# Local attention in half chunks: 64x64 score tiles over 128 keys, global keys apart

## The chip, the cores and the metric

The kernel runs on one core of a Trainium2 chip. The metric is the device time of one launch in microseconds, the median of several runs. TensorE (PE) does the matrix products, VectorE (DVE) and ScalarE (ACT) the elementwise work, and all transfers are issued from the SP queue onto the core's 16 DMA engines.

## What is computed

The reference is one sparse attention followed by two feed-forward layers. The attention has 4 batches, 8 heads, 512 local and 32 global tokens of 64 elements; a local query sees the 32 global keys and the local keys at most 32 positions away, and a global query sees everything:

```python
s_g = scale * q_g @ concat(k_g, k_l).T          # 32 x 544 per head
out_g = softmax(s_g) @ concat(v_g, v_l)
s_ll = where(|i - j| <= 32, scale * q_l @ k_l.T, -1e9)
s_l = concat(scale * q_l @ k_g.T, s_ll)         # 512 x 544, at most 97 of them alive
out_l = softmax(s_l) @ concat(v_g, v_l)
x = concat(out_g, out_l)                        # 2176 tokens x 512
xn = x / rms(x) * rms_g
x = (silu(xn @ w_gate) * (xn @ w_val)) @ w_out  # 512 -> 1536 -> 512
out = (s * relu(x @ w_in)**2 + b) @ w_out2      # 512 -> 2048 -> 512
```

The weights come as float64 and are split into a high and a low float32r part; each feed-forward product is three matmuls (high by high, high by low, low by high).

## The kernel before, in words

The 2176 tokens go through both layers in five groups: three of 512 (the local tokens of batches 0, 1, 2) and two of 320. For each group the main loop goes over 12 slots of the first layer and 16 of the second. `mm3` issues the three matmuls (lines 606 to 608) and is called from `emit_first` (tile m, or m from y) and `emit_second` (tile acc). In the first group's slots the weights are converted beside the products: `conv` takes raw blocks (tile wr), one or two at a time, through ACT and DVE, and the result goes to DRAM (wsc), from where later groups load it.

The attention of batch 0 is done in `start`, before the first products: eight pieces of two chunks (a chunk is 128 queries of two heads), each with `S_` (scores, mask, exponential), `N_` (division by the sum), `T_` (transposes of the probabilities) and `V_` (product with the values). Each piece's queries, keys and values come in one tile s_w. Score and transpose results alternate between the PSUM tiles acc0 and at (two banks each, through `nb`); `V_` takes the one-bank tiles m, of which there are two.

The attention of batches 1 to 3 is cut into 12 units (a batch and two heads), in `unit_steps`. Their steps are queued, and `tick`, called after every group of three matmuls, sends the next one when its time has come. So TensorE's order has short attention groups between long rows of feed-forward matmuls. A unit has two score steps (`sc(0)`, `sc(2)`, line 262), two transpose steps (`st_t`, lines 340 and 341), and one value step (`st_v`, line 354). Every second unit also does the global queries of two units (`st_g` lines 272 and 273, `st_tg` lines 309 and 311, `st_gv` line 329). All of these use one PSUM tile, at, of two banks.

In the score step a chunk's keys are 224 columns: 32 before the chunk, 32 behind it, the 32 global ones, 128 of its own. The two heads lie on partitions 0 to 63 and 64 to 127, so one matmul has 64 rows and 128 output columns, and the heads' results go to different banks. The probabilities, 224 columns a chunk and head, are transposed in two overlapping pieces of 128, and the value step has two matmuls a chunk and head, of 128 rows and 64 output columns each, the two heads side by side. Every float32 matmul of the attention is two instructions on the chip (lines 262, 354, 329, 272, 273); a transpose is one.

The order on each engine is made at build time by a list scheduler with a timing model; `in_turn` keeps a step's matmuls in the order in which they are written.

Of the kernel before, what the change touches and what calls it, by code (L numbers as in the profile page):

```python
# [20 lines left out]
ST = SG + SL  # L21
# [3 lines left out]
KW = 224  # L25
# [30 lines left out]
NMAX = max(GN)  # L56
W_BUFS = 5
# [4 lines left out]
def attn_moe_kernel(ctx: ExitStack, tc: tile.TileContext, s0, q, k, v, w1, w2, cst, out):  # L62
# [47 lines left out]
    pg = cp.tile([128, 64 + ST], F32, name="pg")  # L110
# [104 lines left out]
    def load_u(i):  # L215
        if i >= len(UNITS) or i in raw_u:
            return
        b, p, loc = UNITS[i]
        vr = at_p.tile([128, 4, 2, 2, D], F32, tag="vr", name="vr", bufs=2)
        e = ST if loc else SG  # L220
        qr = at_p.tile([128, ST], F32, tag="qr", name="fq")
        kr = kr_p.tile([128, 4, KW], F32, tag="kr", name="fk")
# [15 lines left out]
    def unit_steps(i):  # L238
# [15 lines left out]
        def sc(c0):  # L254
            qr, kr, vr = raw_u[i]
            bk = banks("at")
            mms = []
            for c in (c0, c0 + 1):
                o = SG + 128 * c
                for h in range(2):  # L260
                    x = slice(64 * h, 64 * h + 64)
                    mms.append(PE.matmul(bk[:, h, (c - c0) * KW:(c - c0 + 1) * KW], lhsT=qr[x, o:o + 128], rhs=kr[x, c]))  # L262
            in_turn(mms)
# [4 lines left out]
        def st_g():  # L268
# [3 lines left out]
            mms = [PE.matmul(bk[64 * e:64 * e + 64, 0], lhsT=qf[:, e], rhs=kr[e][:, :, 96:KW]) for e in range(2)]  # L272
            mms += [PE.matmul(bk[64 * e:64 * e + 64, 1, 0:SG], lhsT=qf[:, e], rhs=kr[e][:, 0, 64:96]) for e in range(2)]
            in_turn(mms)
            neg_scaled(pg[:, 96:96 + SL], bk[:, 0], zw, gm[:, 1:2])
            neg_scaled(pg[:, 64:96], bk[:, 1, 0:SG], zeros[:, 0:SG], gm[:, 0:1])
            V.tensor_tensor(out=gm[:, 2:3], in0=gm[:, 0:1], in1=gm[:, 1:2], op=ALU.min)

        def st_e(cs, g):
# [7 lines left out]
            if g:  # L287
                gm = S["gm"]
                A.activation(out=pg[:, 64:64 + ST], in_=pg[:, 64:64 + ST], func=AF.Exp, scale=-1.0,
                             bias=gm[:, 2:3], accum_out=gm[:, 3:4])  # L290

        def st_r():
# [8 lines left out]
            V.tensor_scalar(out=pg[:, 64:64 + ST], in0=pg[:, 64:64 + ST], scalar1=gm[:, 4:5], scalar2=None, op0=ALU.mult)  # L301

        def st_n(c):
            for h in range(2):
                norm_eng(pm[:, c, h], pm[:, c, h], S["rs"][:, c, h:h + 1], "A" if h else "V")

        def st_tg():
            bk = banks("at")
            mms = [PE.transpose(bk[:, 0, 0:128], pg[:, 0:128], ident)]
            for c in range(4):  # L310
                mms.append(PE.transpose(bk[:, 1, 128 * c:128 * c + 128], pg[:, 96 + 128 * c:224 + 128 * c], ident))
# [7 lines left out]
        def st_gv():  # L319
# [3 lines left out]
            for e in range(2):  # L323
                vr = raw_u[i - 1 + e][2]
                for c in range(5):
                    for h in range(2):
                        o = bk[64 * h:64 * h + 64, SG * e:SG * e + SG]
                        lhs = vr[:, c, 1, h] if c < 4 else vr[:, 0, 0, h]
                        mms.append(PE.matmul(o, lhsT=lhs, rhs=t[:, (c + 1) % 5, e, h], start=(c == 0), stop=(c == 4)))  # L329
# [5 lines left out]
        def st_t(c0):  # L335
            bk = banks("at")
            mms = []
            for c in range(2):
                for h in range(2):
                    mms.append(PE.transpose(bk[:, c, 256 * h:256 * h + 128], pm[:, c0 + c, h, 0:128], ident))  # L340
                    mms.append(PE.transpose(bk[:, c, 256 * h + 128:256 * h + 256], pm[:, c0 + c, h, 96:KW], ident))  # L341
            in_turn(mms)
            t = pt_p.tile([128, 2, 2, 2, 128], F32, tag="pt", name="ptf")
            A.copy(out=t.rearrange("p c h t n -> p c (h t n)"), in_=bk)
            S["pt", c0] = t

        def st_v():
            bk = banks("at")[:, 0]
            vr = raw_u[i][2]
            mms = []  # L350
            for c in range(4):
                for ty in (1, 0):
                    for h in range(2):
                        mms.append(PE.matmul(bk[64 * h:64 * h + 64, 128 * c:128 * c + 128], lhsT=vr[:, c, ty, h],  # L354
                                             rhs=S["pt", c // 2 * 2][:, c % 2, h, ty], start=(ty == 1), stop=(ty == 0)))
            in_turn(mms)
            cpy("V", u_tile(b)[:, p], bk.rearrange("p (c n) -> p c n", c=4))
# [106 lines left out]
    def start():  # L464
# [3 lines left out]
        def ld(i):  # L468
            if not spare:
                t = w_p.tile([128, 2, 1216], F32, tag="w", name="s_w")  # L470
# [3 lines left out]
            rw.append((t[:, 0:256], t[:, 256:704].rearrange("p (c n) -> p c n", c=2),  # L474
                       t[:, 704:1216].rearrange("p (c t h d) -> p c t h d", c=2, t=2, h=2)))
# [20 lines left out]
        G.memset(pg[:, 0:64], 0.0)  # L496
# [13 lines left out]
        def S_(i):  # L510
# [3 lines left out]
            mms = []  # L514
            for c in range(2):
                for h in range(2):
                    x = slice(64 * h, 64 * h + 64)
                    mms.append(PE.matmul(bk[:, h, c * KW:(c + 1) * KW], lhsT=qr[x, 128 * c:128 * c + 128], rhs=kr[x, c]))
            in_turn(mms)
# [9 lines left out]
        def N_(i):  # L529
            V.tensor_scalar(out=st[i][:, 2], in0=st[i][:, 1], scalar1=1e-9, scalar2=None, op0=ALU.add)  # L530
            V.reciprocal(out=st[i][:, 2], in_=st[i][:, 2])
            for n in range(4):
                x = P[i % 4][:, n // 2, n % 2]
                norm_eng(x, x, st[i][:, 2, n:n + 1], "V")

        pts = {}

        def T_(i):
            bk = nb()
            mms = []  # L540
            for c in range(2):
                for h in range(2):
                    mms.append(PE.transpose(bk[:, c, 256 * h:256 * h + 128], P[i % 4][:, c, h, 0:128], ident))
                    mms.append(PE.transpose(bk[:, c, 256 * h + 128:256 * h + 256], P[i % 4][:, c, h, 96:KW], ident))
            in_turn(mms)
            t = pt_p.tile([128, 2, 2, 2, 128], F32, tag="pt", name="s_pt")
            A.copy(out=t.rearrange("p c h t n -> p c (h t n)"), in_=bk)
            pts[i] = t

        def V_(i):  # L550
            bk = one_bank()
            vr = rw[i][2]
            mms = []
            for c in range(2):
                for ty in (1, 0):
                    for h in range(2):
                        mms.append(PE.matmul(bk[64 * h:64 * h + 64, 128 * c:128 * c + 128], lhsT=vr[:, c, ty, h],
                                             rhs=pts[i][:, c, h, ty], start=(ty == 1), stop=(ty == 0)))
            in_turn(mms)
            o = 2 * (i // 4)  # L560
            cpy("A", u_tile(0)[:, i % 4, o:o + 2], bk[:, 0:256].rearrange("p (c n) -> p c n", c=2))
# [145 lines left out]
def _masks():  # L707
    qi = np.arange(128)[:, None]
    m = np.zeros((128, 3, KW), np.float32)
    for t in range(3):  # L710
        pv = np.arange(32)[None] - 32
        nx = np.arange(32)[None] + 128
        ow = np.arange(128)[None]
        m[:, t, 0:32] = np.where((np.abs(qi - pv) <= 32) & (t != 0), 0.0, NEG)
        m[:, t, 32:64] = np.where((np.abs(qi - nx) <= 32) & (t != 2), 0.0, NEG)
        m[:, t, 96:224] = np.where(np.abs(qi - ow) <= 32, 0.0, NEG)
# [3 lines left out]
def _layout(inp):  # L720
# [6 lines left out]
    z = np.zeros((B, HP, 2, 32, D), f)  # L727
    ka = np.zeros((B, HP, 2, 4, KW, D), f)
# [55 lines left out]
```

## Time and profile before

| | us |
|---|---|
| median of 3 runs (lowest, highest) | 1008.27 (1006.88, 1008.33) |
| the profiled execution | 1005.52 |
| its span, first to last instruction | 1003.7 |
| PE busy / DVE busy / ACT busy in the span | 959.5 / 477.5 / 484.2 |

The profile names an instruction by line, engine, operation and tiles (out<-in). Matmuls are pipelined and the record of one reaches past the start of the next, so what a group of matmuls costs is read here from starts: from the start of the last foreign matmul before it to the start of the first one behind it.

### The profile page before, as it was taken

The page shows a single profiled execution, that of the slowest core. Times are in us where ns is not written, and L with a number is a line of the kernel's source. Part 1 is how long each engine was busy: PE and PEld are TensorE (multiplying, and loading weights), DVE is VectorE, ACT ScalarE, POOL GpSimd, SP SyncE. Part 2 cuts the span into 40 slices and gives each one's busy share as a digit, 9 for nine tenths or more (in the row PEclk, how much of TensorE's full clock was granted, in tenths as well). Part 3 has the DMA queues.
Part 4 walks back from the last instruction along what each step waited for, and adds up shares of the span by engine and source line. Part 5 has one row for each costly group of instructions (what it writes and reads, how often), then busy time and mean ns, then how long its engine had stood idle before and what let it go on. Part 6 is the DMA issues. An engine that isn't in the chain of part 4 may idle for free.

```text
span 1003.7 us, 14288 instructions
## 1 busy us (share of the span) xinstructions
PE 959.5 (96%) x5608; PEld 810.5 (81%) x5608; DVE 477.5 (48%) x1117; ACT 484.2 (48%) x906; POOL 0.8 (0%) x9
## 2 busy tenths in 40 slices
PE   6669999899989999999999999999999999999998
PEld 5447878677868878787877878777889999999998
DVE  6995887879854131334254141443252233421323
ACT  6996687768645152544346262643442342321222
POOL 0000000000000000000000000000000000000000
PEclk9888999899999999999999999999999999999999
DMA  9984789768864654436565554436578847898584
GB/s 372 372 299 170 295 336 348 255 222 300 305 222 163 256 191 174 157 132 214 206 222 193 228 192 168 155 130 227 189 263 324 328 170 288 320 371 303 178 328 153
DMA packets 41107, 243.82 MB, mean 243 GB/s; under 512 B 5072, under 2 KB 6096, under 8 KB 23120
## 3 DMA queue, kind: packets, MB, share of 16 engines
q1 hardware_dynamic: 41040, 242.91, 65.4%
q8 instruction: 44, 0.72, 0.3%
q14 instruction: 23, 0.19, 0.1%
HBM read 202.79 MB, written 40.11 MB: 242 GB/s over the span
## 4 chain that ended last, share of the span: by engine, by line
PE 81%; ACT 8%; DMA 5%; DVE 4%; issue 1%; SPq 0%; ACTq 0%; DVEq 0%
PE m L606 14%; PE m L607 14%; PE m L608 14%; PE acc L606 10%; PE acc L607 10%; PE acc L608 10%; DMA wr<-in_w_dram 4%; PE at L354 2%; PE at L262 2%; ACT ce L175 2%; ACT pm L285 2%; ACT cv L174 1%; PE at L340 1%; PE at L329 1%; PE at L341 1%
## 5 line engine op out<-in xcount | busy, mean ns | idle before, releaser
L607 PE MATMUL acc<-h,wt 128*128 128x512 f32 (+1 forms) x560 | 201.5, 361 | 0.0
L608 PE MATMUL acc<-h,wt 128*128 128x512 f32 (+1 forms) x560 | 200.4, 359 | 0.0
L606 PE MATMUL acc<-h,wt 128*128 128x512 f32 (+1 forms) x560 | 191.4, 362 | 0.9 <-DVE y L140 0.6
L606 PE MATMUL m<-x,wt 128*128 128x512 f32 (+2 forms) x496 | 177.7, 359 | 2.6 <-ACT x L134 2.6
L607 PE MATMUL m<-x,wt 128*128 128x512 f32 (+2 forms) x496 | 176.6, 356 | 0.2 <-DVE x L140 0.2
L608 PE MATMUL m<-x,wt 128*128 128x512 f32 (+2 forms) x496 | 176.0, 355 | 0.0
L606 PE MATMUL m<-y,wt 128*128 128x512 f32 (+1 forms) x320 | 116.5, 372 | 7.5 <-ACT y L134 5.1
L606 PEld LDWEIGHTS acc<-h,wt 128*128 128x128 f32 x560 | 103.8, 188 | 16.0 <-issue 1.5
L607 PEld LDWEIGHTS acc<-h,wt 128*128 128x128 f32 x560 | 105.4, 188 | 13.8 <-issue 0.8
L607 PE MATMUL m<-y,wt 128*128 128x512 f32 (+1 forms) x320 | 116.3, 364 | 0.0
L608 PEld LDWEIGHTS acc<-h,wt 128*128 128x128 f32 x560 | 105.4, 188 | 13.2 <-issue 0.2
L608 PE MATMUL m<-y,wt 128*128 128x512 f32 (+1 forms) x320 | 115.7, 362 | 0.0
L676 DVE TENSOR_TENSOR a<-sg,m 128x512 f32<-128x512 f32 (+1 forms) x60 | 36.4, 607 | 150.3 <-PE m L608 132.0
L606 PEld LDWEIGHTS m<-x,wt 128*128 128x128 f32 x496 | 93.9, 190 | 15.7 <-ACT x L134 3.0
L607 PEld LDWEIGHTS m<-x,wt 128*128 128x128 f32 x496 | 94.3, 190 | 12.5 <-issue 1.5
L608 PEld LDWEIGHTS m<-x,wt 128*128 128x128 f32 x496 | 94.3, 190 | 11.4 <-issue 0.8
L695 DVE SCALAR_TENSOR_TENSOR t<-m,ct,r 128x512 f32<-128x512 f32 (+1 forms) x80 | 53.1, 668 | 98.3 <-ACT r L694 97.9
L694 ACT ACTIVATE r<-m 128x512 f32<-128x512 f32 (+1 forms) x80 | 42.0, 532 | 99.6 <-PE m L608 99.3
L697 ACT ACTIVATE h<-t,ct 128x512 fp32r<-128x512 f32 (+1 forms) x80 | 52.4, 659 | 63.2 <-DVE t L695 42.4
L134 ACT CAST h<-a 128x512 fp32r<-128x512 f32 (+1 forms) x60 | 33.3, 555 | 96.6 <-DVE a L676 80.3
L698 DVE SCALAR_TENSOR_TENSOR h<-t,ct,h 128x512 fp32r<-128x512 f32 (+1 forms) x80 | 53.5, 669 | 48.7 <-ACT h L697 48.3
L606 PEld LDWEIGHTS m<-y,wt 128*128 128x128 f32 x320 | 59.9, 190 | 19.9 <-ACT y L134 6.6
(133 smaller groups left out, 1196.2 us busy)
## 6 DMA issues: line engine op xcount, KB each, us to landing
wt<-wsc SPq DMA_DIRECT2D x48, 1536.0 KB, 7.1
wt<-wsc SPq DMA_DIRECT2D x64, 1024.0 KB, 4.8
wr<-in_w_dram SPq DMA_DIRECT2D x68, 512.0 KB, 5.5
wsc<-wt SPq DMA_DIRECT2D x12, 1536.0 KB, 6.1
wsc<-wt SPq DMA_DIRECT2D x16, 1024.0 KB, 5.6
vr<-in_v_dram SPq DMA_DIRECT2D x16, 512.0 KB, 5.6
fk<-in_k_dram SPq DMA_DIRECT2D x16, 448.0 KB, 6.8
s_w<-in_s_dram SPq DMA_DIRECT2D x8, 608.0 KB, 9.9
```

Of the source, the lines that this page charges most:

```text
L134: A.copy(out=out_, in_=in_)
L175: A.copy(out=e.bitcast(I16), in_=odd)
L262: mms.append(PE.matmul(bk[:, h, (c - c0) * KW:(c - c0 + 1) * KW], lhsT=qr[x, o:o + 128], rhs=kr[x, c]))
L285: A.activation(out=pm[:, c, h], in_=pm[:, c, h], func=AF.Exp, scale=-1.0, bias=n2[:, c, h:h + 1], accum_out=S["sum"][:, c, h:h + 1])
L606: PE.matmul(out_, lhsT=wh, rhs=xh, start=first, stop=False)
L607: PE.matmul(out_, lhsT=wh, rhs=xl, start=False, stop=False)
L608: PE.matmul(out_, lhsT=wl, rhs=xh, start=False, stop=last)
L676: V.tensor_tensor(out=a[:, :N], in0=sg[:, :N], in1=vb[:, :N], op=ALU.mult)
L694: A.activation(out=r[:, :N], in_=hb[:, :N], func=AF.Relu)
L695: V.scalar_tensor_tensor(out=t[:, :N], in0=hb[:, :N], scalar=ct[:, C_S:C_S + 1], in1=r[:, :N], op0=ALU.mult, op1=ALU.mult)
L697: A.activation(out=h[:, 0, :N], in_=t[:, :N], func=AF.Identity, bias=ct[:, C_B:C_B + 1])
L698: V.scalar_tensor_tensor(out=h[:, 1, :N], in0=t[:, :N], scalar=ct[:, C_B:C_B + 1], in1=h[:, 0, :N].bitcast(F32), op0=ALU.add, op1=ALU.subt ...
```

## The change

A score tile becomes 64 queries by 160 keys: 128 local keys (32 before the half chunk, its own 64, 32 behind) and the 32 global ones. A chunk of two heads has four such tiles, by half `e` and head `h`; the halves go to different output partitions. The keys are laid out on the host for every half chunk (8 x 160 columns instead of 4 x 224), the values likewise (9 x 128 columns and 64 of the global values instead of 1024), and the local window is one transpose of 128 columns a chunk and head. The global probabilities of two chunks and two heads, 4 x 32 columns, are scaled by the new `glob` and transposed together as a fifth piece. In the value step the local products have 64 moving columns, one a half chunk and head, and the global ones have 32 rows, at four row positions. The value step's result lies in two banks instead of one; in `start` it takes its banks from `nb` instead of m. The piece loaded in `start` grows from 1216 to 1472 columns. The layout of pg (global queries) moves by 64 columns.

```diff
-KW = 224
+KW = 160
+VW = 9 * 128 + 64
+SW = 256 + 4 * KW + 4 * 128 + 64
...
+    def scores(bk, qr, kr, q0, cs):
+        mms = []
+        for n, c in enumerate(cs):
+            for e in range(2):
+                for h in range(2):
+                    x = slice(64 * h, 64 * h + 64)
+                    i = 2 * c + e
+                    mms.append(PE.matmul(bk[64 * e:64 * e + 64, h, n * KW:(n + 1) * KW],
+                                         lhsT=qr[x, q0 + 64 * i:q0 + 64 * i + 64], rhs=kr[x, i]))
+        in_turn(mms)
+
+    def glob(p, rs):
+        gl = pt_p.tile([128, 4, 32], F32, tag="gl", name="gl")
+        V.tensor_tensor(out=gl, in0=p.rearrange("p c h n -> p (c h) n")[:, :, 128:KW],
+                        in1=rs.rearrange("p (n o) -> p n o", o=1).broadcast_to((128, 4, 32)), op=ALU.mult)
+        return gl.rearrange("p n k -> p (n k)")
+
+    def transposes(bk, p, gl):
+        flat = bk.rearrange("p b n -> p (b n)")
+        mms = []
+        for c in range(2):
+            for h in range(2):
+                o = 128 * (2 * c + h)
+                mms.append(PE.transpose(flat[:, o:o + 128], p[:, c, h, 0:128], ident))
+        mms.append(PE.transpose(flat[:, 512:640], gl, ident))
+        in_turn(mms)
+        t = pt_p.tile([128, 5, 128], F32, tag="pt", name="ptf")
+        A.copy(out=t.rearrange("p a n -> p (a n)"), in_=flat[:, 0:640])
+        return t
+
+    def values(bk, vr, vg, pts):
+        mms = []
+        for c in range(2 * len(pts)):
+            t = pts[c // 2]
+            for e in range(2):
+                for h in range(2):
+                    i = 2 * c + e
+                    o = 128 * (c // 2) + 64 * e
+                    mms.append(PE.matmul(bk[64 * h:64 * h + 64, c % 2, o:o + 64],
+                                         lhsT=vr[:, 128 * i + 64 * h:128 * i + 64 * h + 64],
+                                         rhs=t[:, 2 * (c % 2) + h, 64 * e:64 * e + 64], start=(c < 2 and e == 0), stop=False))
+        for c in range(2 * len(pts)):
+            t = pts[c // 2]
+            for h in range(2):
+                x = slice(32 * (2 * (c % 2) + h), 32 * (2 * (c % 2) + h) + 32)
+                o = 128 * (c // 2)
+                mms.append(PE.matmul(bk[64 * h:64 * h + 64, c % 2, o:o + 128], lhsT=vg[x], rhs=t[x, 4],
+                                     start=False, stop=(c // 2 == len(pts) - 1), tile_position=(x.start, 64 * h)))
+        in_turn(mms)
...
         def st_n(c):
+            if not c % 2:
+                S["gl", c] = glob(pm[:, c:c + 2], S["rs"][:, c:c + 2].rearrange("p c h -> p (c h)"))
             for h in range(2):
-                norm_eng(pm[:, c, h], pm[:, c, h], S["rs"][:, c, h:h + 1], "A" if h else "V")
+                norm_eng(pm[:, c, h, 0:128], pm[:, c, h, 0:128], S["rs"][:, c, h:h + 1], "A" if h else "V")
...
         def st_v():
             bk = banks("at")
             vr = raw_u[i][2]
+            values(bk, vr, vr[:, VW - 64:VW], [S["pt", 0], S["pt", 2]])
+            cpy("V", u_tile(b)[:, p].rearrange("p (c b) n -> p c b n", b=2),
+                bk[:, :, 0:256].rearrange("p b (c n) -> p c b n", c=2))
...
         def V_(i):
-            bk = one_bank()
+            bk = nb()
             vr = rw[i][2]
+            values(bk, vr, vr[:, 512:576], [pts[i]])
             o = 2 * (i // 4)
-            cpy("A", u_tile(0)[:, i % 4, o:o + 2], bk[:, 0:256].rearrange("p (c n) -> p c n", c=2))
+            cpy("A", u_tile(0)[:, i % 4, o:o + 2], bk[:, :, 0:128])
```

## Rows read from the trace of the kernel before

**Rows 1.** The page: PE's busy share, and PE's granted clock in 40 slices.

```profile
PE 959.5 (96%) x5608; PEld 810.5 (81%) x5608; DVE 477.5 (48%) x1117; ACT 484.2 (48%) x906; POOL 0.8 (0%) x9
PEclk9888999899999999999999999999999999999999
```

**Rows 2.** Windows: stretch, length, busy PE, PEld, DVE, ACT, POOL, clock, DMA, GB/s.

```profile
20.00:40.00 20.00, 13.87 (x126) 10.02 (x124) 19.95 (x78) 17.97 (x45) 0.00 (x0) 1.00 1.03 413
...
60.00:80.00 20.00, 12.16 (x61) 9.56 (x60) 19.65 (x54) 18.22 (x40) 0.00 (x0) 0.76 0.84 312
...
460.00:560.00 100.00, 100.00 (x515) 80.68 (x512) 38.67 (x82) 43.48 (x77) 0.00 (x0) 1.00 0.60 219
```

**Rows 3.** Timeline of PE, a value step between products: start, length, instruction, count.

```profile
403.49 0.39 PE L608 MATMUL m<-x,wt 128*128 128x512 f32 x1
403.72 0.39 PE L606 MATMUL m<-x,wt 128*128 128x512 f32 x1
404.04 1.97 PE L354 MATMUL at<-ptf,vr 128*64 128x128 f32 x32
405.93 0.50 PE L607 MATMUL m<-x,wt 128*128 128x512 f32 x1
```

**Rows 4.** Timeline of PE, a transpose step, the first and the last of eight.

```profile
397.60 0.27 PE L340 MATMUL at<-ct,pm 128*128 128x128 f32 x1
...
398.36 0.27 PE L341 MATMUL at<-ct,pm 128*128 128x128 f32 x1
```

**Rows 5.** Timeline of PE, a score step between products.

```profile
410.82 0.39 PE L607 MATMUL m<-x,wt 128*128 128x512 f32 x1
411.14 1.03 PE L262 MATMUL at<-fk,fq 64*128 64x224 f32 x8
412.10 0.50 PE L608 MATMUL m<-x,wt 128*128 128x512 f32 x1
```

**Rows 6.** Timeline of PE, a value step of the global queries between products.

```profile
475.97 0.39 PE L607 MATMUL m<-y,wt 128*128 128x512 f32 x1
476.29 1.36 PE L329 MATMUL at<-pgt,vr 128*64 128x32 f32 x40
477.58 0.50 PE L608 MATMUL m<-y,wt 128*128 128x512 f32 x1
```

**Rows 7.** Groups by form: line, engine, operation, shapes, count | busy us, mean ns | idle before.

```profile
L229 DVE CUSTOM_DVE_ANT_0 pm<-at,ct 128x224 f32<-128x224 f32 x108 | 35.7, 385 | 37.8 <-PE at L262 37.8
...
L236 DVE TENSOR_SCALAR pm<-pm,rs 128x224 f32<-128x224 f32 x48 | 13.1, 331 | 0.3
...
L547 ACT COPY s_pt<-acc 128x1024 f32<-128x1024 f32 x7 | 7.0, 995 | 1.3 <-PE acc L544 1.3
...
L229 DVE CUSTOM_DVE_ANT_0 pg<-at,zeros 128x512 f32<-128x512 f32 x8 | 5.4, 679 | 3.9 <-PE at L273 3.9
...
L316 ACT COPY pgt<-at 128x512 f32<-128x512 f32 x8 | 4.7, 592 | 0.0
...
L301 DVE TENSOR_SCALAR pg<-pg,gm 128x544 f32<-128x544 f32 x8 | 4.0, 502 | 0.2
...
L444 DVE TENSOR_TENSOR nt<-nt,msq 128x512 f32<-128x512 f32 x2 | 1.4, 692 | 0.1
...
L444 DVE TENSOR_TENSOR nt<-nt,msq 128x256 f32<-128x256 f32 x2 | 0.8, 414 | 0.0
```

**Rows 8.** The chain that ended last, its first part: start, length, what.

```profile
12.64 11.14 DMA wr<-in_w_dram
23.79 10.74 DMA wr<-in_w_dram
...
36.31 1.05 ACT cv L174
```

**Rows 9.** Timeline of PE, a stall inside two score steps.

```profile
291.41 1.03 PE L262 MATMUL at<-fk,fq 64*128 64x224 f32 x8
296.05 1.22 PE L262 MATMUL at<-fk,fq 64*128 64x224 f32 x8 [3.61 <-DVE nm L229]
```

More of the change, by code (lines that the diff above doesn't have):

```diff
@@ L256, in sc @@
             bk = banks("at")
[L257 to L263, printed above, removed]
+            scores(bk, qr, kr, SG, (c0, c0 + 1))
             for h in range(2):
@@ L324, in st_gv @@
                 vr = raw_u[i - 1 + e][2]
[L325 removed]
+                for a in range(5):
                     for h in range(2):
                         o = bk[64 * h:64 * h + 64, SG * e:SG * e + SG]
[L328 to L329 removed]
+                        w = 128 * min(2 * a, 8) + 64 * h
+                        mms.append(PE.matmul(o, lhsT=vr[:, w:w + 64], rhs=t[:, a, e, h], start=(a == 0), stop=(a == 4)))
             in_turn(mms)
@@ L335, in st_t, with st_v @@
         def st_t(c0):
+            S["pt", c0] = transposes(banks("at"), pm[:, c0:c0 + 2], S["gl", c0])
+        def st_v():
             bk = banks("at")
[L337 to L348, printed above, removed]
-            vr = raw_u[i][2]
[L350 to L357, printed above, removed]
+            vr = raw_u[i][2]
+            values(bk, vr, vr[:, VW - 64:VW], [S["pt", 0], S["pt", 2]])
+            cpy("V", u_tile(b)[:, p].rearrange("p (c b) n -> p c b n", b=2),
+                bk[:, :, 0:256].rearrange("p b (c n) -> p c b n", c=2))
             load_u(i + 1)
@@ L513, in S_ @@
             bk = nb()
[L514 to L519, printed above, removed]
+            scores(bk, qr, kr, 0, (0, 1))
             for h in range(2):
@@ L531, in N_ @@
             V.reciprocal(out=st[i][:, 2], in_=st[i][:, 2])
+            gls[i] = glob(P[i % 4], st[i][:, 2])
             for n in range(4):
-                x = P[i % 4][:, n // 2, n % 2]
+                x = P[i % 4][:, n // 2, n % 2, 0:128]
                 norm_eng(x, x, st[i][:, 2, n:n + 1], "V")
         pts = {}
+        gls = {}
         def T_(i):
[L539 to L547, printed above, removed]
+            t = transposes(nb(), P[i % 4], gls[i])
             pts[i] = t
         def V_(i):
-            bk = one_bank()
+            bk = nb()
             vr = rw[i][2]
[L553 to L559, printed above, removed]
+            values(bk, vr, vr[:, 512:576], [pts[i]])
             o = 2 * (i // 4)
-            cpy("A", u_tile(0)[:, i % 4, o:o + 2], bk[:, 0:256].rearrange("p (c n) -> p c n", c=2))
+            cpy("A", u_tile(0)[:, i % 4, o:o + 2], bk[:, :, 0:128])
         bs = [build_steps(0, 0), build_steps(0, 1)]
```

75 lines of the change are left out of this document (38 added, 37 removed).

## The prediction

> **What bounds the kernel now.** First the page: TensorE is busy for 96% of the span and its granted clock is full but for a few slices [rows 1]. Then the windows, to see where this holds. In the opening it does not: PE works 12 to 14 us of every 20, while DVE is busy for 19.95 and 19.65 of 20 [rows 2]. Later it does: from 460 to 560 us PE is busy for all of the 100 us, and DVE for 38.7, ACT for 43.5 [rows 2]. So an attention step of the later stages costs what it takes of PE, and DVE and ACT cost nothing there; in the opening it is the other way round. Eleven of the twelve units have their steps after the opening, so eleven is the factor below.
>
> Then the timeline of PE, for what a step costs. I read it from starts. A product matmul of 512 columns follows its predecessor after 0.23 us (403.49 to 403.72). Round the value step the distance is 405.93 - 403.72 = 2.21, so the step costs 2.21 - 0.23 = 1.98 us [rows 3]. A float32 transpose of 128 columns takes (398.36 - 397.60) / 7 = 0.109 us, 0.85 ns a column [rows 4]; eight take 0.87. At that price the 32 instructions of the value step, 128 columns each, would need 3.5 us one by one, and 16 x 0.109 = 1.74 two by two. So the two heads, whose outputs lie side by side, run together, and 1.98 - 1.74 = 0.24 us is what the array loses on entering and leaving the narrower tile form.
>
> The score step costs 412.10 - 410.82 - 0.23 = 1.05 us [rows 5]: 224 columns are 0.19, four pairs 0.76, and 0.29 remain, the 0.24 and 0.05 more. Here the heads lie on different rows, and they too run two by two. The global value step costs 477.58 - 475.97 - 0.23 = 1.38; without 0.24 that is 1.14 for 20 pairs, 57 ns a pair, though 32 columns would stream in 27 [rows 6]. So a pair with new weights of 64 columns has a floor of 57 ns.
>
> **The change, part by part, in the later stages.**
>
> *Transposes.* Five a step for eight: 3 x 0.109 = 0.33 us less, two steps a unit, 0.66 less. Nothing is added on PE.
>
> *Scores.* Sixteen instructions of 160 columns (0.136 us each) for eight of 224. They form four tiles, two row halves by two column halves. If the four run abreast there are four slots: 4 x 0.136 + 0.24 = 0.78, 0.27 less than 1.05. If only two run together there are eight: 1.33, 0.28 more. No row shows four tiles, nor two that differ in both directions. The nearest rows show each direction by itself at its full worth: rows in the score step, columns in the value step. I take four abreast: 0.54 less a unit. The other end, 0.56 more, stays for the range.
>
> *Values.* The local part keeps its 32 instructions, with 64 columns for 128. 64 columns stream in 55 ns, so the floor of 57 holds: 16 x 0.057 = 0.91. The global part is new: 16 instructions of 128 columns with 32 rows each, at four row positions and two column halves. Four abreast they take 4 x 0.109 = 0.44, two abreast 0.87, one by one 1.74. Between the two parts the tile form changes once more; I take half of the 0.24, 0.12, with 0 and 0.24 as its ends. With entry and exit the step is 0.91 + 0.44 + 0.24 + 0.12 = 1.71, against 1.98 now: 0.27 less; two abreast 2.14, 0.16 more; one by one 3.01, 1.03 more. I take four abreast, since each of the four positions has its own rows.
>
> A rule speaks against that choice. The Trainium skill, "TensorEngine Tiling (Array Packing)", section "Restrictions and Gotchas", says that different row tiles cannot access the same PSUM bank at the same time. The two heads of a chunk have different row positions and one bank here. By that rule the global part would go two abreast; no run here shows it yet. In the score step the row halves have banks of their own, so the rule leaves it alone.
>
> *Sum.* A unit takes 0.54 + 0.66 + 0.27 = 1.47 us less of PE; eleven units, 16.2 us. The switch's ends are 1.3 us either way.
>
> *What lies beside it.* A masked score pass on DVE goes from 224 to 160 columns: (679 - 385) / 288 = 1.02 ns a column, so 65 ns less. A normalisation goes from 224 to 128: (502 - 331) / 320 = 0.53, 51 less. The new `glob` has 128 elements: (692 - 414) / 256 = 1.09, so 414 - 139 = 275 ns. ACT's copy of the transposes goes from 1024 to 640 columns: (995 - 592) / 512 = 0.79, 302 less [rows 7]. A unit's DVE work is 8 x 65 + 4 x 51 - 2 x 275 = 174 ns less, so `glob` is paid for, though it now stands between the reciprocal and the transposes. DVE at 39% covers that delay; without cover it would be 2 x 0.275 a unit, 6 us in all. The global queries' steps keep their counts. Keys and values of a unit bring 288 KB more, 16 times, 4.7 MB, on a queue whose engines are at 0.60 of their time there [rows 2].
>
> **The opening.** Work on the two full engines falls. DVE: eight rounds of 4 x 65 + 4 x 51 - 275 = 189 ns, and the first unit's 174, 1.7 us in all. ACT: eight copies, 2.4 us, besides shorter exponentials. Transfers grow. Eight pieces have 128 KB more each, two units 288 KB each, the constants 96 KB less: 1.5 MB, at 413 GB/s [rows 2] 3.7 us. On the SP queue they stand ahead of the raw weight blocks, which follow one another without a break to 34.53 us, and the conversion that needs some of them starts at 36.31 [rows 8]. So at least 1.8 of the 3.7 us are covered, and up to 1.9 are not. The first piece also comes 0.3 us later.
>
> A wait is added too. `V_` leaves its own two tiles for the two that `S_` and `T_` share: three uses a round instead of two. The scores of piece i+3 now wait until ACT has copied out the value product of piece i, and behind them on PE's queue stand the next transposes, for which ACT and DVE wait. DVE's conversion work can fill such gaps only where it stands ahead in its order. I put the opening at 1.7 less, 1.9 + 0.3 more, and 0.5 for this wait, 1 us more in all; its ends are 2 less and 8 more (a microsecond in each of eight rounds).
>
> The sum is made against the profiled execution, 1005.5 us, a span of 1003.7 and 1.8 around it: 1005.5 - 16.2 + 1 = 990.3. The median is 2.8 above that execution, so the forecast for the median is 1008.3 - 16.2 + 1 = 993.1.
>
> **The rivals.**
>
> *The global products go two abreast.* A unit saves 0.54 + 0.66 - 0.16 = 1.04, eleven 11.4: 1008.3 - 11.4 + 1 = 997.9. For it: no row shows row tiles that share a bank. Against it: the heads of the value step share a bank already, at different output partitions [rows 3].
>
> *Tiles overlap only where they share their rows or their columns.* Every overlap in the trace is of that kind: the scores' pairs share all columns, the values' pairs all rows [rows 3, 5]. Then the scores go in pairs, and the global products one by one, as each next tile differs in both. A unit pays 0.56 - 0.66 + 1.03 = 0.93 more, eleven 10.2: 1008.3 + 10.2 + 1 = 1019.5, slower. It decides from five slots a score step on (2 x (5 x 0.136 + 0.24 - 1.05) - 0.66 + 1.03 is above zero). Against it: each direction alone costs nothing. The Trainium skill, "TensorE: Matmul & The Clock Gate", section "Part 3: Packing small matmuls", has rows and columns compose, at 10.6 times the rate for 16 tiles; no row here shows it, and by it the time would be the forecast's.
>
> *Scores and global products both in pairs.* 0.56 - 0.66 + 0.16 = 0.06 more a unit: 1008.3 + 0.7 + 1 = 1010.0, no change.
>
> *The opening pays its 8 us.* 993.1 + 7 = 1000.1. For it: the added waits lie where no slack is on DVE. Against it: three uses of two tiles fit into rounds of over 6 us.
>
> Beside all of these stand stalls like that of 3.6 us between two score steps, where the second waits until DVE has read the first one's banks [rows 9]: a new order on the engines can lose one or make one, some 4 us either way.
>
> **How the numbers follow.** Forecast 0.46; global products in pairs 0.22; overlap in one direction only 0.09; both in pairs 0.09; the late opening 0.10; other mishaps 0.04. The likeliest case's own range is 986 to 1000 (stall 4, opening and switch 3 together). The range for 8 in 10 goes from 985 to 1010: it takes in all but the overlap in one direction, the mishaps and the tails. A measurement of this kernel tells 0.2%, 2 us, from no change. Faster: the forecast, the first rival and the late opening, less a little for stalls, 0.76. Same: 0.09. Slower: 0.15.
>
> **What would show it.** In the changed kernel a score step should cost 0.78 between products (1.33 if in pairs), with four starts close together; a transpose step five starts 0.109 apart; a value step 1.71 (2.14, 3.01). PE should become dense at about the same time as now, about 1 us later. I am wrong if the score step costs more than 1.05, if the value step's second part takes over 0.9, if the steps come apart into more pieces, each with its own entry and exit, or if PE becomes dense several microseconds later.

## The result and the profile after

The changed kernel takes 995.51 us (median of 4 runs, 994.65 to 997.97) against 1007.58 for the kernel before on the same chip: a ratio of 0.9891 [0.9862, 0.992], 12.1 us faster. The forecast was 993.1. Three repetitions on other occasions, below, gave 0.9913, 0.9886 and 0.9884, 9 to 11 us. So the gain is real, about 1% of the time, and some 3 to 6 us smaller than the 15.2 of the sum. The profiled execution took 997.97 us, the longest of the four.

First the page after (busy time and share of each engine, and PE's granted clock in 40 slices), to be laid beside [rows 1]:

```profile
PE 946.3 (95%) x6024; PEld 790.7 (79%) x6024; DVE 471.7 (47%) x1149; ACT 464.9 (47%) x908; POOL 0.8 (0%) x9
...
PEclk9578999999999999999999999999999999999999
```

PE has 416 instructions more and is busy for 13.2 us less. Then the windows of [rows 2], with the same columns:

```profile
20.00:40.00 20.00, 15.96 (x143) 9.77 (x141) 18.33 (x74) 14.14 (x41) 0.00 (x0) 0.61 1.02 413
60.00:80.00 20.00, 6.92 (x56) 5.02 (x55) 19.43 (x56) 15.60 (x37) 0.00 (x0) 0.64 1.00 386
460.00:560.00 100.00, 100.00 (x539) 79.60 (x539) 35.71 (x73) 41.00 (x75) 0.00 (x0) 1.00 0.60 218
```

The limits stand where they stood: PE is full from 460 to 560 us, DVE nearly full in the opening.

Next PE's timeline after, a score step, a transpose step and a value step, each with a product before and behind it, as in [rows 3 to 5]:

```profile
353.28 0.39 PE L624 MATMUL m<-x,wt 128*128 128x512 f32 x1
353.60 0.77 PE L237 MATMUL at<-fk,fq 64*64 64x160 f32 x16
354.31 0.50 PE L622 MATMUL m<-x,wt 128*128 128x512 f32 x1
...
390.06 0.39 PE L622 MATMUL m<-x,wt 128*128 128x512 f32 x1
390.30 0.60 PE L253 MATMUL at<-ct,pm 128*128 128x128 f32 x4
390.73 0.27 PE L254 MATMUL at<-ct,gl 128*128 128x128 f32 x1
390.76 0.48 PE L623 MATMUL m<-x,wt 128*128 128x512 f32 x1
...
401.66 0.39 PE L623 MATMUL m<-x,wt 128*128 128x512 f32 x1
401.98 1.15 PE L268 MATMUL at<-ptf,vr 128*64 128x64 f32 x32
403.06 0.67 PE L276 MATMUL at<-ptf,vr 32*64 32x128 f32 x16
403.66 0.50 PE L624 MATMUL m<-x,wt 128*128 128x512 f32 x1
```

From starts, less the product's own 0.23 us: the score step costs 354.31 - 353.28 - 0.23 = 0.80 us (forecast 0.78; 1.05 before), the transpose step 390.76 - 390.06 - 0.23 = 0.47 (0.80 before by the same reading; the 0.33 between them is the three transposes forecast), the value step 403.66 - 401.66 - 0.23 = 1.77 (forecast 1.71; 1.98 before). The second part of the value step, 16 instructions of 128 columns, takes 403.66 - 403.06 = 0.60 with the way out of the tile form. One by one they would take 1.74, two abreast 0.87: four run abreast. In the trace the single starts come in fours within 21 ns, 0.136 us from one four to the next in the score step and 0.109 in the global products; the local products come in pairs, 58 ns apart.

DVE's and ACT's forms (busy, mean ns of one | idle before), beside [rows 7]:

```profile
L281 DVE CUSTOM_DVE_ANT_0 pm<-at,ct 128x160 f32<-128x160 f32 x104 | 27.6, 321 | 32.8 <-PE at L237 32.8
L257 ACT COPY ptf<-at 128x640 f32<-128x640 f32 x27 | 18.6, 689 | 26.3 <-PE at L254 26.3
...
L288 DVE TENSOR_SCALAR pm<-pm,rs 128x128 f32<-128x128 f32 x48 | 11.7, 282 | 0.0
L243 DVE TENSOR_TENSOR gl<-pm,rs 128x128 f32<-128x128 f32 x24 | 6.9, 288 | 0.2
```

These give 385 - 321 = 64 ns less a masked pass (forecast 65), 331 - 282 = 49 a normalisation (51), 995 - 689 = 306 a copy (302), and 288 for `glob` (275).

So every price was right within 0.06 us, and the missing microseconds must lie between the steps. Both kernels have the same 4128 product matmuls, so the start of the n-th one tells how far a kernel has come. In microseconds from the span's start:

| product | before | after | third control | control less before |
|---|---|---|---|---|
| 145th | 104.7 | 102.0 | 101.5 | -3.2 |
| 421st | 174.1 | 173.6 | 173.1 | -1.0 |
| 465th | 187.4 | 184.2 | 183.7 | -3.7 |
| 505th | 206.6 | 207.8 | 206.8 | +0.2 |
| 865th | 310.0 | 309.7 | 309.3 | -0.7 |
| 1001st | 341.7 | 342.9 | 342.4 | +0.7 |
| 2401st | 725.5 | 715.2 | 714.7 | -10.8 |
| last | 999.9 | 991.8 | 989.8 | -10.1 |

The third control is the changed kernel again; its profiled execution took 995.41 us. From the 1001st to the 2401st product the changed kernel gains 11.5 us, and every other profile of this order the same within 0.2 us (the price of the steps in that stretch says 11.2). At the 1001st it has gained nothing. The first group of tokens has passed both layers by then (its last product is the 864th), and the second group has begun. What is lost on the way is lost in two places: from the 465th to the 505th product, and from the 865th to the 1001st.

### The profile page after: what moved, and what is told of

The parts are those of the page before. It is cut to its first block, busy times and chain, and to the rows that moved or that the text cites. A ratio compares the mean times of both kernels' runs of the same rounds, so it can differ in the third digit from the quotient of the medians.

```text
span 995.6 us, 15191 instructions
## 1 busy us (share of the span) xinstructions
PE 946.3 (95%) x6024; PEld 790.7 (79%) x6024; DVE 471.7 (47%) x1149; ACT 464.9 (47%) x908; POOL 0.8 (0%) x9
## 4 chain that ended last, share of the span: by engine, by line
PE 80%; DMA 7%; DVE 6%; ACT 5%; issue 1%; SPq 0%; ACTq 0%; DVEq 0%
PE m L622 15%; PE m L624 14%; PE m L623 14%; PE acc L622 10%; PE acc L623 10%; PE acc L624 10%; DMA wr<-in_w_dram 4%; DMA wt<-wsc 2%; PE at L237 2%; PE at L268 1%; ACT ce L177 1%; PE at L377 1%; PE at L253 1%; DVE wt L142 1%; DMA fq<-in_q_dram 1%
## 5 line engine op out<-in xcount | busy, mean ns | idle before, releaser
L623 PEld LDWEIGHTS m<-x,wt 128*128 128x128 f32 x496 | 93.9, 189 | 10.8 <-DVE x L142 0.8
L685 ACT ACTIVATE sg<-m 128x512 f32<-128x512 f32 (+1 forms) x60 | 32.0, 534 | 96.9 <-PE m L624 96.7
L622 PEld LDWEIGHTS m<-y,wt 128*128 128x128 f32 x320 | 59.8, 189 | 20.8 <-ACT y L136 4.4
L713 ACT ACTIVATE h<-t,ct 128x512 fp32r<-128x512 f32 (+1 forms) x80 | 52.2, 658 | 50.9 <-DVE t L711 33.1
## 6 DMA issues: line engine op xcount, KB each, us to landing
s_w<-in_s_dram SPq DMA_DIRECT2D x8, 736.0 KB, 11.5
```

Source lines behind the costliest of these rows:

```text
L622: PE.matmul(out_, lhsT=wh, rhs=xh, start=first, stop=False)
L623: PE.matmul(out_, lhsT=wh, rhs=xl, start=False, stop=False)
L685: A.activation(out=sg[:, :N], in_=gb[:, :N], func=AF.Silu)
L713: A.activation(out=h[:, 0, :N], in_=t[:, :N], func=AF.Identity, bias=ct[:, C_B:C_B + 1])
```

## The experiments

**Is it PE's time?** The theory of the prediction: a microsecond of an attention step on PE is a microsecond of the kernel. Against it, that PE has slack and the gain comes from DVE or ACT. The changed kernel gets three useless transposes more a step (their results are never read), beside a control that is the changed kernel itself.

> The changed kernel once more, as the mark for the others of this call. Theory (eleven units save 14 to 16 us of PE, the opening gives 2 us, the first group's stage gives some back in stalls): 995 us, ratio 0.988. The rival (the first four runs were a lucky order of stalls) has it at 998 or more, ratio over 0.991.

996.82 us (996.21 to 1001.14), ratio 0.9913 [0.9893, 0.9932].

> The changed kernel with three transposes more in each transpose step (the fifth one repeated into unused columns), so that the step has eight as before. It measures what a microsecond of PE is worth in the whole. Theory (after the opening PE time counts in full): a step costs 0.80 us instead of 0.47, and 22 to 24 steps of 0.33 us make the kernel 7 to 8 us slower than the control. Rival (in the first group's stage the conversions on DVE and ACT set the pace, so part of the PE time saved there is worth nothing): 4 to 5 us slower, and the stalls of that stage shrink.

```diff
         mms.append(PE.transpose(flat[:, 512:640], gl, ident))
+        for o in (640, 768, 896):
+            mms.append(PE.transpose(flat[:, o:o + 128], gl, ident))
```

1003.8 us (1001.84 to 1006.96), ratio 0.9976 [0.9963, 0.9989], 7.0 us over the control. That is the number of the theory, but not for its reason. The edit stands in a function that the eight pieces of the opening call too, so 32 steps have three transposes more (96 PE instructions more on the page, 6120 for 6024), not 22 to 24, and at 0.33 us a step they ask for 10.5 us. The starts of the products tell where they count. From the 1001st to the 2401st product this run takes 377.0 us and the control with no edit 372.3: 4.7 us for fourteen steps, which ask for 4.6. The 145th product starts at 105.7 us, in the unedited runs at 101.3 to 102.1: 3.6 us or more for the ten steps ahead of it, which ask for 3.3. Between the 145th and the 1001st stand eight steps, 2.6 us, and there nothing is seen of them: 240.3 us, where the unedited profiles of this order have 238.2 to 244.5. So PE's time counts in full from the 1001st product on. In the first group's stage the added time is lost among stalls that vary more than it does. That fits the rival; that conversions set the pace there is not shown by it.

**Do the shared banks cost something?** In `start` the value products now use the banks that scores and transposes alternate on. Here they have two of their own again, at the price of a second copy.

> The changed kernel with the value step of the opening back on tiles of its own (two one-bank tiles m, two copies instead of one), so that scores and transposes have acc0 and at to themselves as before. Theory (the added wait costs half a microsecond; DVE and ACT set the opening): within 1 us of the control, PE dense at the same time, the extra copies costing ACT 8 x 0.16 = 1.3 us. Rival (the shared banks cost the opening about a microsecond a round): 3 to 8 us faster.

```diff
-            bk = nb()
+            bk = [one_bank(), one_bank()]
...
-            cpy("A", u_tile(0)[:, i % 4, o:o + 2], bk[:, :, 0:128])
+            for c in range(2):
+                cpy("A", u_tile(0)[:, i % 4, o + c], bk[c][:, 0:128])
```

997.15 us (995.06 to 997.28), ratio 0.9903 [0.9885, 0.9921]: as the control. So the wait does not cost the 8 us of the prediction's late opening; the 0.5 us of its sum are less than these medians can tell.

**How do four tiles come to run abreast?** The program names the four tiles in turn. Here it names all matmuls of one tile, then those of the next.

> The changed kernel with the matmuls of a score step written tile by tile: all four instructions of one quarter of the array (two chunks, two passes each), then those of the next, where the changed kernel goes round the quarters. It asks how four tiles come to run together. Theory (each quarter takes its instructions as a stream of its own, and TensorE sees 16 instructions ahead): a score step still costs 0.80 us and the kernel is within 1.5 us of the control. Rival (tiles run together only where their instructions stand next to each other): a step costs up to 16 x 0.136 + 0.24 = 2.4 us, and the kernel is up to 22 x 1.6 = 35 us slower; anything between tells how far it sees.

```diff
-        for n, c in enumerate(cs):
-            for e in range(2):
-                for h in range(2):
+        for e in range(2):
+            for h in range(2):
+                for n, c in enumerate(cs):
```

995.87 us (995.28 to 996.31), ratio 0.989 [0.9876, 0.9903]. Its score step on PE's timeline:

```profile
354.36 0.39 PE L624 MATMUL m<-x,wt 128*128 128x512 f32 x1
354.68 0.80 PE L237 MATMUL at<-fk,fq 64*64 64x160 f32 x16
355.40 0.50 PE L622 MATMUL m<-x,wt 128*128 128x512 f32 x1
```

355.40 - 354.36 - 0.23 = 0.81 us, as before the edit. So the order of issue inside a step hardly matters here: a tile does not wait for another tile's instruction that stands ahead of it in these 16.

**Do the added transfers eat the rest?** The kernel before, with copies of the added size in memory behind its own loads of values and pieces (they are written back to memory, and nothing reads them).

> The kernel before with the bytes that the change adds, and nothing else of it: behind each of the eight pieces of the opening a transfer of 128 KB, and behind the loads of each of the 12 local units one of 288 KB, from DRAM to DRAM and read by nobody. Theory (what the first group's stage gives back comes from transfers that push the raw weight blocks later): 2 to 5 us slower than the kernel before, with ACT's waits for raw blocks before 300 us, 4.4 us there, at 8 or more. Rival (the bytes are hidden, the given-back time is the new order's): within 1 us.

```diff
         raw_u[i] = (qr, kr, vr)
+        if loc:
+            pad = dr_p.tile([128, 576], F32, name=f"pad{i}")
+            nc.sync.dma_start(out=pad, in_=v[b, p].rearrange("p c t h d -> p (c t h d)")[:, 0:576])
...
             nc.sync.dma_start(out=t, in_=s0[i])
+            pad = dr_p.tile([128, 256], F32, name=f"spad{i}")
+            nc.sync.dma_start(out=pad, in_=s0[i, :, 0:256])
```

1009.36 us (1007.27 to 1012.71), ratio 1.0025 [1.0015, 1.0034]: 2.2 us. The start of the first product into acc in the kernel before, in the changed one, and here:

```profile
93.00 0.40 PE L606 MATMUL acc<-h,wt 128*128 128x512 f32 x1
```

```profile
90.73 0.40 PE L622 MATMUL acc<-h,wt 128*128 128x512 f32 x1
```

```profile
99.34 0.40 PE L611 MATMUL acc<-h,wt 128*128 128x512 f32 x1
```

The time is the theory's, the place is not. Of the lateness of this profiled execution, which is the longest of its eleven, 6.3 us stand already here, out of 7.4 at the last product. From the 421st to the 1001st product it took 168.1 us, the kernel before 167.6, and ACT's waits for raw blocks before 300 us, which were to be 8 or more, are 4.3. So bytes alone do not explain the first group's missing gain. In the changed kernel, which has such bytes, the opening is not late; but its ACT waits 14.9 us for raw blocks before 300 us (line 176, the same conversion), and why is not shown.

**The wait for the global queries.** Of the missing gain, most is missing from the 421st to the 1001st product. In the kernel before that stretch holds 3 value steps, 6 score steps and 5.1 transpose steps, in the changed one 3.4, 6 and 7; at the measured prices it should take 2.2 us less, 165.4 for 167.6. It took 169.3, 3.9 more. What PE waited for, from 184 to 212 us, where the first group goes from the first layer to the second: before, and after (waits in total, times, the longest; y is the second layer's input, made in halves by ACT and DVE):

```profile
PE m L606 <- ACT y L134: 2.6, 1, 2.6
PE acc L606 <- DVE y L140: 0.6, 1, 0.6
PE m L606 <- DVE t L695: 0.3, 1, 0.3
```

```profile
PE m L623 <- DVE y L142: 2.9, 2, 2.1
PE m L622 <- ACT y L136: 1.9, 2, 1.0
PE acc L623 <- DVE h L142: 1.0, 1, 1.0
PE at L237 <- DVE nm L281: 0.6, 1, 0.6
PE at L237 <- DVE u L138: 0.5, 1, 0.5
PE acc L622 <- DVE y L142: 0.3, 1, 0.3
```

3.5 us have become 7.2. By starts the difference is smaller, 3.2 us from the 465th to the 505th product beyond the price of the steps there (2.7 in the third control), since the kernel before loses time there without waiting: from 196 to 202 us its granted clock is 0.57, after it is 1.00 there and 0.79 in the next 6 us. The largest wait, 2.1 us for DVE's part of y, is explained in part by DVE's timeline after, with what ended its idle time in brackets:

```profile
202.45 0.37 DVE L300 COPY qf<-fq 64x32 f32<-64x32 f32 x2 [0.81 <-DMA fq<-in_q_dram]
202.84 1.22 DVE L189 SCALAR_TENSOR_TENSOR cv<-wr,cv 128x1024 int32<-128x1024 int32 x1
...
204.10 0.64 DVE L142 TENSOR_TENSOR y<-acc,y 128x512 fp32r<-128x512 f32 x1
```

DVE stands 0.81 us before its copies of the next unit's global queries until the load of fq lands, and y is queued behind, as is a conversion of 1.22 us. (The load takes 8.16 us, from the end of the last score step at 194.26; DVE works through nearly all of them. So the 8 us of the next expectation are the load's, not a stand of DVE.) That tile has one buffer: its load can start only when the score steps have read the last one, and these stand later here than in the kernel before. So the global queries get a tile of their own, with two buffers.

```diff
+        qg = at_p.tile([128, SG], F32, tag="qg", name="fg", bufs=2)
+        qr = at_p.tile([128, SL], F32, tag="qr", name="fq")
...
+        nc.sync.dma_start(out=qg, in_=q[b, p, :, 0:SG])
+        if loc:
+            nc.sync.dma_start(out=qr, in_=q[b, p, :, SG:ST])
```

> The changed kernel with the 32 global queries of a unit loaded into a small tile of their own with two buffers, so that the copies into qf wait for 16 KB that come early and not for the whole query tile, which has one buffer and is loaded only after the last scores of the unit before. In the profile of the changed kernel this wait holds DVE for 8 us near 194 us, PE stands for 5 us of it. Theory: that stall is the part that the first group's stage gives back; it goes, and the kernel gets 3 to 5 us faster than the control. Rival (the transfers as a whole are late there, and the next wait, on raw weight blocks, takes its place): within 1.5 us of the control.

995.3 us (993.22 to 1001.58), ratio 0.9904 [0.9877, 0.993], beside the first control's 996.82.

> The version with the global queries in a tile of their own once more, beside a control on the same chip, as 1.5 us between medians was too little to tell. Theory: 1 to 3 us faster than the control, in the first group's stage alone. Rival: no difference, the order of the medians was chance.

994.3 us (992.84 to 998.12), ratio 0.9882 [0.9864, 0.9899], beside this control:

> The changed kernel, the mark for this call: 995 to 997 us, ratio 0.989 to 0.992.

996.22 us (992.3 to 996.95), ratio 0.9886 [0.9869, 0.9902]. Both times the edit is 1.5 to 1.9 us below its control, and both times the intervals overlap: a likely gain of 1 to 2 us, not a settled one, and not the 3 to 5 that were expected first. In the profiles the stretch from the 421st to the 1001st product took 166.6 and 166.8 us with it; without it 169.3, 173.0, 166.7, 170.5, 169.1 and 169.3 in the six executions with this order. One of the six is as short as those with the edit, so the profiles do not settle it either. DVE's copy of qf no longer waits, and PE's waits for DVE's y fall from 2.9 us in total to 1.8 in the first run of this version and, shown here, 0.8 in the second:

```profile
PE m L625 <- DVE y L142: 0.8, 1, 0.8
```

All of PE's waits from 184 to 212 us fall less, from 7.2 us to 7.0 and 6.2, as others stand in their place; the second control has 6.7.

**Where the steps meet the layer change.** How the order of the steps changed is visible first at the end of the opening. PE's timeline before, the first and largest of three pieces of the first unit's value step:

```profile
81.51 1.83 PE L354 MATMUL at<-ptf,vr 128*64 128x128 f32 x26
```

and after:

```profile
101.73 0.33 PE L268 MATMUL at<-ptf,vr 128*64 128x64 f32 x2
...
110.37 0.33 PE L268 MATMUL at<-ptf,vr 128*64 128x64 f32 x2
...
117.66 1.03 PE L268 MATMUL at<-ptf,vr 128*64 128x64 f32 x28
118.63 0.67 PE L276 MATMUL at<-ptf,vr 32*64 32x128 f32 x16
```

The step, and a score step of the second unit, now lie behind the first products into acc. From there on the steps stand elsewhere against the products: the score steps of the third unit (the second in the expectations below) fall behind the 474th and the 476th product, on the layer change itself, where the kernel before had them behind the 448th and the 468th. Two ways to turn that round: pace the first group's steps earlier in the changed kernel, and later in the kernel before.

```diff
-            sched["end"] = sched["t"] + 0.95 * tot
+            sched["end"] = sched["t"] + (0.87 if gi == 0 else 0.95) * tot
```

> The changed kernel once more, as the measure for the next two. 996 us (995 to 997.5). Between the 465th and the 505th product, where the first group goes from its first to its second layer, about 10 us beyond the products and the attention steps' own cost, as in the five runs with this order so far (9.2 to 11.5); the kernel before has 5.3 there.

994.98 us (993.32 to 995.41), ratio 0.9884 [0.9871, 0.9897]. From the 465th to the 505th product it has 10.1 us beyond the products (0.2275 us each) and the price of the steps. By the same reading the kernel before has 7.5 there and not 5.3, so what is missing at the layer change is 2.7 us, not more than 4.

> The changed kernel with one number altered: the first group's attention steps are spread over 0.87 of its time for 0.95, so that the second unit's score steps stand ahead of the layer change again, as in the kernel before, and its exponentials no longer stand, eight in a row, ahead of the last of the four copies of y on ACT. If the missing 4 us are the price of that meeting: stalls there fall from about 10 to 5 or 6, and the time to 992 us (990.5 to 993.5). If they come from the later loads or from chance, or if a stall of the same size comes up elsewhere: 996, as the control.

1000.44 us (999.16 to 1002.09), ratio 0.994 [0.9927, 0.9953]: 5.5 us slower than the control, where 4 faster were expected. PE's waits from 276 to 304 us:

```profile
PE at L237 <- DVE nm L281: 3.7, 1, 3.7
PE at L237 <- DVE msq L476: 2.6, 1, 2.6
PE m L622 <- DVE t L711: 1.9, 1, 1.9
```

At the layer change the waits for y are all but gone (0.2 us), and others stand in their place: 3.2 us for ACT's h, 1.2 for its copy of the transposes, 1.0 for the masked passes. With the score steps back where the kernel before has them, behind the 440th and the 468th product, the 465th to the 505th product have the same 2.7 us over the kernel before, beyond the price of their steps, as in the third control. So moving them did not give it back. The larger loss is new: at 278 us both score steps of a later unit meet the normalisation of the second group. Its chain on ACT and DVE (msq and what follows) stands ahead of the masked passes that free the score banks, and PE waits 8.2 us in these 28, where the third control waits 2.9 and the kernel before 3.6 [rows 9].

> The same, and the 32 global queries in a tile of their own with two buffers, so that their copies on DVE wait for no load that has to wait for the score steps. If both causes are real and apart: 990.5 us (989 to 992). If the wait for the queries cost only where it met the layer change: 992, as the run with the pace alone.

1001.08 us (999.65 to 1002.88), ratio 0.9947 [0.9935, 0.9959]: as the run with the pace alone. With this order the queries' own tile gains nothing.

> The kernel before with 1.03 for 0.95: its second unit's score steps now stand at the layer change (in the order of the program behind the 474th and the 488th product), where the changed kernel has its own, but its exponentials behind all four copies of y. If score steps at the layer change cost by themselves, DVE's passes standing ahead of its part of y: slower, 1010 to 1012 us. If what costs there is only the exponentials ahead of the copies of y: faster by the 2.6 us that y waits for ACT in the kernel before, 1004 to 1005 us. If neither matters: 1007.

1012.57 us (1009.99 to 1014.22), ratio 1.006 [1.0046, 1.0074], 6.3 us slower. The time is what the first alternative named, its mechanism is not. PE's longest wait at the layer change:

```profile
204.28 0.80 PE L606 MATMUL m<-y,wt 128*128 128x512 f32 x1 [5.18 <-DVE t L695]
```

The kernel before, with its score steps as late as the changed one has them, has the wait for the queries too: DVE waits 2.75 us for them, and t, for which PE waits, is queued behind and starts at 203.48 (ACT's r, which t needs as well, came late too, at 201.60). In its own order the load had landed before DVE came to the copies.

Yet the time is not lost there. The 465th to the 505th product take 17.7 us, in the kernel before 19.2, and at the 865th product, at 310.7 us, the run is 0.7 us behind it. At the 1001st, at 350.3 us, it is 8.5 us behind, and so it ends. In that stretch the second group begins, and steps of a unit that the slower pace has left over, which the kernel before has behind the 816th product, stand at its first products:

```profile
308.93 1.86 PE L262 MATMUL at<-fk,fq 64*128 64x224 f32 x8 [2.97 <-DVE nm L229]
...
321.62 0.80 PE L606 MATMUL m<-x,wt 128*128 128x512 f32 x1 [2.13 <-ACT sg L669]
```

The granted clock is 0.59 from 310 to 315 us, 0.60 from 320 to 325 and 0.72 from 325 to 330, where the kernel before has 1.00 from 310 on. So this run loses at another place than the one it was made for, and does not say what score steps at the layer change cost.

**Steps in pieces.** The second place of the table, from the 865th to the 1001st product, costs the changed kernel 33.1 us where the kernel before needs 31.7, in every profile of this order, and the price of the steps there is the same, 0.7 us in both. PE waits for nothing in it. What stands there is one unit's value step, in five pieces:

```profile
313.93 0.45 PE L268 MATMUL at<-ptf,vr 128*64 128x64 f32 x6
...
320.63 0.56 PE L268 MATMUL at<-ptf,vr 128*64 128x64 f32 x10
...
324.07 0.33 PE L268 MATMUL at<-ptf,vr 128*64 128x64 f32 x2
...
329.31 0.33 PE L268 MATMUL at<-ptf,vr 128*64 128x64 f32 x2
...
346.80 0.57 PE L268 MATMUL at<-ptf,vr 128*64 128x64 f32 x12
```

From the starts round them the pieces cost 0.46, 0.58, 0.35, 0.34 and, with the global part, 1.19 us: 2.92 for a step that costs 1.77 in one. The four ahead of the 1001st product cost 1.73 for the 0.74 that their 20 instructions would take in one row, 1.0 us more. In the run with three more transposes the step came in three pieces, which cost 2.34 us, and the stretch took 32.1. No run here kept the step together on purpose.

## Why the prediction was right, and where it was off

**What bounds the kernel**: right where the gain lies. From the 1001st product on PE's time counts at its full price (three transposes more a step: 4.7 us for 4.6). In the first group's stage it was not seen to count: eight such steps, 2.6 us, left no mark.

**The prices of the steps**: right, all three. The two choices that had no row, four tiles abreast and global products four abreast, came out as taken. The rivals "in pairs", "overlap in one direction only" and "both in pairs" are out: they needed 1.33 us a score step or 0.87 and more for the global products. The rule of the Trainium skill, "TensorEngine Tiling (Array Packing)", section "Restrictions and Gotchas", that different row tiles cannot access one PSUM bank at the same time, is not borne out here: the two heads of a chunk, on different rows and different output partitions of one bank, started within 21 ns of each other. Row tiles with the same output partitions were not tried. That rows and columns compose, as the Trainium skill, "TensorE: Matmul & The Clock Gate", section "Part 3: Packing small matmuls", has it, agrees with 0.80 us a score step.

**The factor eleven**: off by one for two of the three steps, since a value step and a score step moved from the opening to behind the first products. Twelve value steps at 1.77, 22 score steps at 0.80 and 22 transpose steps at 0.47 stand against 11, 20.8 and 22 at 1.99, 1.05 and 0.80.

**The opening**: forecast 1 us later. The first product into acc came 2.3 us earlier, and the moved steps, 2.34 + 0.80, are paid behind it: 0.9 us later in all. That this is near the forecast is partly luck: that these steps would leave the opening was not foreseen, and its terms were not measured one by one. The late opening as a rival is out; its added wait for banks cost nothing that could be measured.

**The stalls**: here the forecast missed. They stood at nothing in the sum, with 4 us either way beside it, and so did steps in pieces, which the prediction named as a sign of being wrong. In the table the third control is 3.2 us ahead at the 145th product; the steps from there on should bring 12.2 more, 15.4 in all, against 10.1 found. 3.9 of the 5.3 us that are missing lie between the 421st and the 1001st product: 169.3 us for the 165.4 worked out above. In the third control 2.7 of them lie at the layer change, from the 465th to the 505th product, and 1.3 behind the 865th, where PE waits for nothing and a value step comes in five pieces. With the first unit's value step, also in pieces (0.57 us), steps in pieces make about 1.6 of the 5.3. At the layer change it is shown that PE's waits are others and longer than before. That DVE's wait for the global queries is a part of them, 1 to 2 us in the medians, is likely and not settled. What the layer change is worth by itself is not shown: the same order gave 1.3 us in place of 3.9 in the second control's profile and 7.6 in the first's, and each other pace tried lost more elsewhere. The 0.8 us that are left are no larger than the differences between executions.

**What would have told it beforehand**: the row was there, in kind. [rows 9] is such a stall, and the prediction's own remark that a new order can lose one or make one holds. What it left out is that steps which shrink also move every later step against the products. A step in pieces was in that trace too: a value step of 14, 4 and 14 instructions behind the 516th product, which from starts costs 2.69 us for 1.99. Which steps would break up, or which waits would grow, could not be read from the trace of before.

## What to carry to other kernels

Price an attention or side step by the starts of the instructions around it; prices built so held here within 0.06 us, even for a tile form that no row showed. Then ask where the shorter steps will stand against the places at which one engine's queue holds the next layer's input, and whether they stay in one piece: here 2.7 of 15.4 us were lost at such a place and about 1.6 to value steps in pieces, and pacing the first group's steps earlier or later lost more at another place. A small operand that many steps need early, like 32 global queries, may gain from a buffer of its own, apart from a large one that is released late; here that gave 1.5 and 1.9 us in the medians, within their noise. And when an added load is to tell what time is worth, count every place that runs it, and look where in the kernel the time appears: a total can come out right for another reason.

## What the runs showed of the hardware

Four tiles of 64 rows by 64 columns run abreast, in both orders of issue that were tried (0.80 and 0.81 us for 16 instructions of 160 columns), and so do four tiles of 32 rows by 64 columns (16 instructions of 128 columns start in fours 0.109 us apart), with two tiles writing different partitions of one bank.

In the opening PE's granted clock stood lower than before: 0.61 from 20 to 40 us with 15.96 us busy, against 1.00 with 13.87 [rows 2]. The busy time does not say that PE had more to do, as the same instruction takes longer at the lower level. Two pairs of products of 256 columns on PE's timeline after show the two levels:

```profile
79.63 0.41 PE L624 MATMUL m<-x,wt 128*128 128x256 f32 x1
79.84 0.41 PE L622 MATMUL m<-x,wt 128*128 128x256 f32 x1
...
83.10 0.28 PE L622 MATMUL m<-x,wt 128*128 128x256 f32 x1
83.22 0.28 PE L623 MATMUL m<-x,wt 128*128 128x256 f32 x1
```

0.21 us from start to start is 1.2 GHz, 0.12 is 2.4. Before the work of the first pair began, at 77.70 us, PE had stood idle for 8.4 us; the level rose, near 82.6 us, after it had worked with one break of 0.11 us. What the lower level cost in the opening was not measured; DVE is busy there for 18.33 and 19.43 of 20 us.
